# A tail check of tiny weights in place of zeroing them, and a wider spread of the rounding of the four later weights

## The chip, the core and the metric

The kernel runs on one core of one Trainium2 chip. Its engines work in parallel, each through its own queue in a fixed order: TensorE (PE, with its weight loads shown apart as PEld), VectorE (DVE), ScalarE (ACT), GpSimd (POOL), and SyncE (SP), whose queue issues every DMA of this kernel. The metric is the device time of one execution in microseconds (us), the median of the runs.

## The reference

Four batches of 768 positions with 8 heads of width 48 (384 channels) go through three layers, each of which needs the whole output of the one before.

```python
for t in range(S):                                   # gated linear attention
    state = sigmoid(f_logit[:, :, t, :, None]) * state + outer(k[:, :, t], v[:, :, t])
    y[:, :, t] = q[:, :, t] @ state

h = np.maximum(x @ w_in, 0)                          # 384 -> 1024, halves u and v of 512
v_n = (v - mean(v)) / sqrt(var(v) + 1e-06)           # over the 512 channels
gated = u * (w_spatial @ v_n + b_spatial)            # mixes the 768 positions
x = gated @ w_out                                    # 512 -> 384

h = np.maximum(x.T @ w_tok1, 0) @ w_tok2             # token layers, 768 -> 256 -> 768
u = x + h.T
out = u + np.maximum(u @ w_ch1, 0) @ w_ch2           # channel layers, 384 -> 1536 -> 384
```

Six of the weights (`w_in`, `w_out`, `w_tok1`, `w_tok2`, `w_ch1`, `w_ch2`) arrive as 64-bit floats, all else as 32-bit floats. Products are made to nearly full 32-bit precision: each factor is split into a high and a low part, and three matmuls are added up.

## The kernel before

**Stages.** `body` computes everything. For each batch `att` does the attention (scans on DVE, lines 228 to 319; 8 units of two heads a batch, named `pg` and `fkq` by their tiles), `s1` the first product and the normalisation, and `s23` the mixing over positions and the product with `w_out`. The attention of the next batch is woven between the steps of this one (`weave`). After the fourth batch come the token layers (`c1`, `c2`) and the channel layers (`ff`), again batch by batch: `up1` makes 9 matmuls into a PSUM tile, ACT writes its high part `hh` (line 641), DVE its low part `hl` (line 642), and `down` uses both in 9 matmuls (line 654). There are 12 such steps in each of 8 halves, `ff(b, 0)` and `ff(b, 1)`; the latter also has the token layers of the next batch between its steps.

**Rounding the wide weights.** `rounded` (line 58) makes 32-bit floats of a piece of 128 rows by up to 384 columns. A DMA fetches the piece as pairs of 32-bit words (384 KB; line 61, tiles `...st`, ring of three buffers). DVE puts together the new word in two steps (lines 66 and 69), ACT scales the low word (line 73), POOL adds it (line 74). Then ACT squares the high word read as a float (line 75), and DVE multiplies the result with 0 where that square lies under a bound (line 79), so that weights too small for this way of rounding become zero. There are 47 pieces: 9 of `w_in` and 4 of `w_out`, split at once by `split_weight`, and 34 of the four later weights, which `round_weight` writes to a buffer in DRAM (line 93); `split_weight` fetches them again later (line 120, tiles `...sa`).

**The gate.** Attention divides by running products of the gates. Each unit leaves the products in `pend` (line 239). After the last one, DVE takes the least of them (lines 550 to 556) and sets `flag` if it lies under a bound. At the end all engines read the flag; if it is set, `body(True)` does the whole work again in a slower, safe way. With these inputs it is not set.

**Order.** The order of the code is not the order of the queues. Python calls give a stream of instructions; the framework's scheduler then places them by a model of the engines, each as soon as its operands, its buffer and its engine are free there, with code order as a priority. The queues that result are fixed, and an engine that waits for an instruction holds everything behind it.

Of the kernel before, what the change touches and what calls it, by code (L numbers as in the profile page):

```python
# [18 lines left out]
def tile_kernel(ctx, tc, fkqs, v, w_in, w_sp, b_sp, w_out, w_t1, w_t2, w_c1, w_c2, out):  # L19
    nc = tc.nc  # L20
    B, S, DM = v.shape
    P = 128
# [29 lines left out]
    nhalf = const.tile([P, 1], F32, name="nhalf")  # L52
    pend = const.tile([P, B * NP, NCH], F32, name="pend")


    LEAST = 3.4332275390625e-05 ** 2

    def rounded(stage, a, src, c0, width, name):

        st = stage.tile([P, WST, 2], U32, tag="wst", name=f"{name}st")  # L60
        nc.sync.dma_start(
            out=st[:, :width, :].rearrange("p c t -> p (c t)"), in_=src[:, 2 * c0 : 2 * (c0 + width)]
        )
        yield
        lo, hi = st[:, :width, 0], st[:, :width, 1]
        nc.vector.tensor_scalar(
            out=a, in0=hi, scalar1=3, scalar2=0x3FFFFFFF, op0=ALU.logical_shift_left, op1=ALU.bitwise_and
        )
        nc.vector.scalar_tensor_tensor(
            out=a, in0=hi, scalar=0xC0000000, in1=a, op0=ALU.bitwise_and, op1=ALU.bitwise_or  # L70
        )

        nc.scalar.activation(lo, lo, AF.Copy, scale=2.0**-29)
        nc.gpsimd.tensor_tensor(out=a, in0=a, in1=lo, op=ALU.add)
        nc.scalar.activation(f32(hi), f32(hi), AF.Square)
        yield

        a = f32(a)
        nc.vector.scalar_tensor_tensor(out=a, in0=f32(hi), scalar=LEAST, in1=a, op0=ALU.is_ge, op1=ALU.mult)
        return a  # L80

    def round_weight(stage, src, name):

        if src.dtype != mybir.dt.uint64:
            return src, []
        rows, cols = src.shape
        dst = dram.tile([rows, cols], F32, name=name + "d")
        srcr = src.bitcast(U32).rearrange("(n p) c -> n p c", p=P)

        def piece(i, c0, width):  # L90
            at = stage.tile([P, WST], U32, tag="wsa", name=f"{name}da{i}{c0}")
            a = yield from rounded(stage, at[:, :width], srcr[i], c0, width, f"{name}d{i}{c0}")
            nc.sync.dma_start(out=dst[i * P : (i + 1) * P, c0 : c0 + width], in_=a)

        return dst, [
            partial(piece, i, c0, min(WST, cols - c0)) for i in range(rows // P) for c0 in range(0, cols, WST)
        ]

    kept = {}

    def split_weight(pool, stage, src, name, n, cols, eng, first=0, order=None, psum=None):

        wide = src.dtype == mybir.dt.uint64
        h = pool.tile([P, n, cols], F32R, name=name + "h")
        l = pool.tile([P, n, cols], F32R, name=name + "l")
        if wide:
            src = src.bitcast(U32)
        srcr = src.rearrange("(n p) c -> n p c", p=P)

        def piece(i, c0, width):  # L110
            sl = (slice(None), i, slice(c0, c0 + width))
            at = stage.tile([P, WST], U32, tag="wsa", name=f"{name}sa{i}{c0}")
            a = at[:, :width]
            if wide:
                a = yield from rounded(stage, a, srcr[first + i], c0, width, f"{name}{i}{c0}")
                nc.scalar.copy(h[sl], a)
                yield
            else:
                a = f32(a)
                nc.sync.dma_start(out=a, in_=srcr[first + i][:, c0 : c0 + width])  # L120
                yield
                nc.scalar.copy(h[sl], a)
                yield
                yield
            if eng is not nc.tensor:
                eng.tensor_tensor(out=l[sl], in0=a, in1=f32(h[sl]), op=ALU.subtract)
                return

            ps = psum.tile([P, W], F32, tag="m", name=f"{name}pl{i}{c0}")[:, :width]
            nc.tensor.matmul(ps, ident, a, start=True, stop=False)  # L130
            nc.tensor.matmul(ps, minus, h[sl], start=False, stop=True)
            yield
            nc.scalar.copy(l[sl], ps)

        where = [(i, c0, min(WST, cols - c0)) for i in range(n) for c0 in range(0, cols, WST)]
        return h, l, [partial(piece, *x) for x in (order(where) if order else where)]

    def staged(pieces):

        gens = []  # L140

        def step(n):
            if n < len(pieces):
                gens.append(pieces[n]())
            for g in gens[max(0, n - 4) : n + 1]:
                next(g, None)

        return [partial(step, n) for n in range(len(pieces) + 4)]

    def weave(main, *fillers):  # L150

# [14 lines left out]
    def body(general):  # L166
# [12 lines left out]
        wl = lp("wl", 1)  # L179
# [15 lines left out]
        ps_m = lp("ps_m", 3, space=PSUM, st=whole)  # L195
# [10 lines left out]
        first, last = (attp.tile([P, W], F32, name=x) for x in ("first", "last"))  # L206
# [249 lines left out]
        def s23(b):  # L456
# [39 lines left out]


        winh, winl, steps = split_weight(
            wr, wst, w_in, "win", NK, DFF, nc.tensor, order=lambda x: sorted(x, key=lambda y: -y[1]), psum=ps_m
        )  # L500
        weave(att(half(0, 0)), staged(steps))
        bb = const.tile([P, S], F32, tag="bb", name="bb")
        nc.sync.dma_start(out=bb, in_=b_sp.unsqueeze(0).to_broadcast([P, S]))
        wsph, wspl, st_a = split_weight(wl, wst, w_sp, "wsp", NCH, S, nc.tensor, psum=ps_m)
        wouth, woutl, st_b = split_weight(wl, wst, w_out, "wout", NJ, DM, nc.tensor, psum=ps_m)
# [6 lines left out]
        if not general:  # L512
            for name, src in (("wt1", w_t1), ("wt2", w_t2), ("wc1", w_c1), ("wc2", w_c2)):
                kept[name], x = round_weight(wst, src, name)
                early += x
            early = staged(early)
        part = lambda n: early[len(early) * n // 5 : len(early) * (n + 1) // 5]
        for b in range(B - 1):
            if b:
                weave(s1(b, 0), rest)  # L520
            a, rest = s1(b, 1), []
            m, rest = s23(b)
            steps = att(half(b + 1, 0) + half(b + 1, 1))
            cut = len(steps) * len(a) // len(a + m)
            weave(a, steps[:cut], out_steps if b == 0 else part(2 * b - 1))
            weave(m, steps[cut:], part(2 * b))
        right.close()
        wr2 = ExitStack()
        w2p = wr2.enter_context(tc.tile_pool(name="w2p", bufs=1, side="right"))
# [1 line left out]
        t2h, t2l, st_b = split_weight(w2p, wst, kept["wt2"], "wt2", NT1, S, nc.gpsimd)  # L531
        c1h, c1l, st_c = split_weight(w2p, wst, kept["wc1"], "wc1", NK - 1, DC, nc.gpsimd)
        c1w = [(c1h[:, c, :], c1l[:, c, :]) for c in range(NK - 1)]
        weave(rest + s1(B - 1, 0) + s1(B - 1, 1), staged(st_a + st_b))
        conv = st_c
        mid.close()
        w2q = wr2.enter_context(tc.tile_pool(name="w2q", bufs=1, side="right"))
# [10 lines left out]
        if not general:  # L548

            nc.vector.tensor_reduce(  # L550
                out=least, in_=pend.rearrange("p u c -> p (u c)"), op=ALU.min, axis=mybir.AxisListType.X
            )
            row = ps_s.tile([P, W], F32, tag="s", name="row")[:1, :P]
            nc.tensor.transpose(row, least, ident)
            nc.vector.tensor_reduce(out=least[:1], in_=row, op=ALU.min, axis=mybir.AxisListType.X)
            nc.vector.tensor_scalar(out=flag, in0=least[:1], scalar1=LOW, scalar2=None, op0=ALU.is_lt)
# [132 lines left out]
        h3p = e(tc.tile_pool(name="h3p", bufs=4))  # L689
        op = e(tc.tile_pool(name="op", bufs=2))  # L690
        otp = e(tc.tile_pool(name="otp", bufs=3))
        c2h, c2l, st_c = split_weight(w3p, wst, kept["wc2"], "wc2", NF, DM, nc.vector)
        st_c = staged(by_block[2 * NK : 3 * NK] + st_c[:3] + by_block[3 * NK :] + st_c[3:])
        weave(c2(0), st_c[:12])
        for b in range(B):
            more = []
            if b + 1 < B:
                ld, mm = c1(b + 1)
                weave(ff(b, 0), ld, st_c[12:] if b == 0 else [])
                more = mm + c2(b + 1)  # L700
            else:
                weave(ff(b, 0))
            weave(ff(b, 1), more)
        ph2.close()
        wr2.close()
        whole.close()
# [54 lines left out]
```

## Time and profile before

| | us |
|---|---|
| median of three runs | 821.85 (820.16 to 822.72) |
| the profiled execution | 819.0 |
| its span, first to last instruction | 817.2 |

| engine | busy in the span, us | share |
|---|---|---|
| PE | 777.3 | 95% |
| PEld | 716.3 | 88% |
| DVE | 420.3 | 51% |
| ACT | 289.1 | 35% |
| POOL | 211.1 | 26% |

The granted clock of TensorE was 0.978 of full speed over the span. The stages lie about as follows: attention and first layers up to 405 us, the rest of the fourth batch and the first token layers up to 465, channel layers from there to 809. Matmuls are pipelined, so the time of one, as a row prints it, is longer than the distance between two; a busy PE is not PE at its peak. Busy time of weight loads (PEld) shows the density better. A row of the chain of waits names the work that ended last before the next could begin.

### The profile page before, as it was taken

The page shows a single profiled execution, that of the slowest core. Times are in us where ns is not written, and L with a number is a line of the kernel's source. Part 1 is how long each engine was busy: PE and PEld are TensorE (multiplying, and loading weights), DVE is VectorE, ACT ScalarE, POOL GpSimd, SP SyncE. Part 2 cuts the span into 40 slices and gives each one's busy share as a digit, 9 for nine tenths or more (in the row PEclk, how much of TensorE's full clock was granted, in tenths as well). Part 3 has the DMA queues.
Part 4 walks back from the last instruction along what each step waited for, and adds up shares of the span by engine and source line. Part 5 has one row for each costly group of instructions (what it writes and reads, how often), then busy time and mean ns, then how long its engine had stood idle before and what let it go on. Part 6 is the DMA issues. An engine that isn't in the chain of part 4 may idle for free.

```text
span 817.2 us, 12758 instructions
## 1 busy us (share of the span) xinstructions
PE 777.3 (95%) x4860; PEld 716.3 (88%) x4860; DVE 420.3 (51%) x820; ACT 289.1 (35%) x649; POOL 211.1 (26%) x265
## 2 busy tenths in 40 slices
PE   5899899898989999999999999999999999999996
PEld 3577688688779888899899999999999999999995
DVE  6968599899898846673552532122122212221211
ACT  5766464555553444231632531122111211221110
POOL 4524344555641212110760330004000400010000
PEclk9899899999999999999999999999999999999998
DMA  7563435766474321220441410002000200000000
GB/s 254 176 207 104 147 96 164 236 225 214 146 237 140 101 96 59 65 67 24 128 126 40 138 56 30 1 4 85 1 30 0 87 1 30 1 8 24 30 1 33
DMA packets 39847, 73.74 MB, mean 90 GB/s; under 512 B 5216, under 2 KB 29664, under 8 KB 39776
## 3 DMA queue, kind: packets, MB, share of 16 engines
q1 hardware_dynamic: 39776, 72.83, 27.7%
q8 instruction: 40, 0.66, 0.3%
q14 instruction: 31, 0.25, 0.1%
HBM read 54.72 MB, written 15.73 MB: 86 GB/s over the span
## 4 chain that ended last, share of the span: by engine, by line
PE 71%; DVE 10%; DMA 10%; issue 4%; ACT 2%; SPq 1%; POOL 1%; DVEq 0%; ACTq 0%; POOLq 0%
PE po L654 19%; PE p L164 8%; PE p L162 8%; PE p L163 8%; DMA fkq<-in_fkq 3%; PE ps L162 3%; PE ps L164 3%; PE ps L163 3%; PE pa L259 2%; PE py L309 2%; PE py L315 2%; PE px L162 2%; PE px L163 1%; PE px L164 1%; DVE pg L236 1%
## 5 line engine op out<-in xcount | busy, mean ns | idle before, releaser
L642 DVE SCALAR_TENSOR_TENSOR hl<-p,hh 128x384 fp32r<-128x384 f32 x96 | 53.3, 557 | 188.4 <-ACT hh L641 188.4
L641 ACT ACTIVATE hh<-p 128x384 fp32r<-128x384 f32 x96 | 47.2, 492 | 198.0 <-PE p L164 198.0
L654 PE MATMUL po<-hl,wc2h 128*128 128x384 f32 x288 | 97.3, 338 | 0.0
L654 PE MATMUL po<-hh,wc2l 128*128 128x384 f32 x288 | 96.7, 336 | 0.0
L665 POOL TENSOR_TENSOR us<-uh,ul 128x384 f32<-128x384 f32 x24 | 24.3, 1024 | 232.0 <-DVE ul L625 214.7
L654 PE MATMUL po<-hh,wc2h 128*128 128x384 f32 x288 | 75.0, 336 | 0.0
L162 PE MATMUL ps<-wsph,vh 128*128 128x384 f32 x192 | 67.5, 351 | 0.0
L163 PE MATMUL ps<-wspl,vh 128*128 128x384 f32 x192 | 66.4, 346 | 0.0
L164 PE MATMUL ps<-wsph,vl 128*128 128x384 f32 x192 | 66.1, 346 | 0.0
L164 PE MATMUL p<-uh,wc1l 128*128 128x384 f32 x192 | 65.0, 338 | 0.0
L264 POOL TENSOR_SCALAR_AFFINE_SELECT am<-am 128x384 f32<-128x384 f32 x64 | 46.9, 748 | 69.7 <-ACT am L263 69.5
L163 PE MATMUL p<-ul,wc1h 128*128 128x384 f32 x192 | 64.7, 337 | 0.0
L162 PE MATMUL p<-uh,wc1h 128*128 128x384 f32 x192 | 64.2, 338 | 0.0
L654 PEld LDWEIGHTS po<-hl,wc2h 128*128 128x128 f32 x288 | 54.1, 188 | 0.1
L654 PEld LDWEIGHTS po<-hh,wc2l 128*128 128x128 f32 x288 | 54.1, 188 | 0.0
L654 PEld LDWEIGHTS po<-hh,wc2h 128*128 128x128 f32 x288 | 52.3, 188 | 0.0
L236 DVE TENSOR_TENSOR_SCAN pg<-fs,first 128x384 f32<-128x384 f32 x32 | 33.3, 1039 | 22.2 <-ACT first L379 22.1
L259 PE MATMUL pa<-fkq 48*128 48x128 f32 x384 | 40.6, 316 | 3.0 <-ACT am L263 3.0
L259 PEld LDWEIGHTS pa<-fkq 48*128 48x128 f32 x384 | 30.5, 204 | 12.3 <-issue 4.3
L162 PEld LDWEIGHTS ps<-wsph,vh 128*128 128x128 f32 x192 | 37.1, 193 | 2.4 <-issue 1.6
L625 DVE TENSOR_TENSOR ul<-p,uh 128x384 fp32r<-128x384 f32 x24 | 13.4, 557 | 47.6 <-ACT uh L624 47.6
L163 PEld LDWEIGHTS ps<-wspl,vh 128*128 128x128 f32 x192 | 37.0, 193 | 0.5 <-issue 0.2
(419 smaller groups left out, 1928.5 us busy)
## 6 DMA issues: line engine op xcount, KB each, us to landing
fkq<-in_fkq SPq DMA_DIRECT2D x31, 578.0 KB, 4.5
vt<-in_v SPq DMA_DIRECT2D x8, 576.0 KB, 5.9
x1d<-xs SPq DMA_DIRECT2D x24, 192.0 KB, 2.0
xf<-x1d SPq DMA_DIRECT2D x12, 384.0 KB, 4.5
out<-ot SPq DMA_DIRECT2D x24, 192.0 KB, 2.0
wspsa<-in_w_sp SPq DMA_DIRECT2D x12, 192.0 KB, 2.6
wc1d<-wc1da SPq DMA_DIRECT2D x12, 192.0 KB, 2.4
wc2d<-wc2da SPq DMA_DIRECT2D x12, 192.0 KB, 2.2
```

Of the source, the lines that this page charges most:

```text
L162: nc.tensor.matmul(ps, lh, rh, start=first and i == 0, stop=False, **kw)
L163: nc.tensor.matmul(ps, lh, rl, start=False, stop=False, **kw)
L164: nc.tensor.matmul(ps, ll, rh, start=False, stop=i == n - 1, **kw)
L236: nc.vector.tensor_tensor_scan(out=pc, data0=fs[:, :W], data1=first, initial=0.0, op0=ALU.mult, op1=ALU.add)
L259: nc.tensor.matmul(pa[j][:, c, :], ki[64 * j : 64 * j + D, sl], qi[64 * j : 64 * j + D, sl], start=True, stop=True)
L264: nc.gpsimd.affine_select(out=am[j], in_=am[j], compare_op=ALU.is_ge, fill=0.0, base=0, pattern=[[0, NCW], [1, C]], channel_multiplier=-1,)
L309: nc.tensor.matmul(py[:112, c, :], now[c][:112, :112], qi[:112, c * C : (c + 1) * C], start=c == 0, stop=False, skip_group_check=True,)
L315: nc.tensor.matmul(py[64 * j : 64 * j + m, c, :], vt[:, c, h0 + D * j : h0 + D * j + m], am[j][:, c, :], start=False, stop=True, skip_grou ...
L641: nc.scalar.activation(hh, ps, AF.Relu)
L642: nc.vector.scalar_tensor_tensor(out=hl, in0=ps, scalar=0.0, in1=f32(hh), op0=ALU.max, op1=ALU.subtract)
L654: nc.tensor.matmul(po[c], l[:, ft, csl], r, start=ft == 0 and x == 0, stop=ft == NF - 1 and x == 2)
L665: nc.gpsimd.tensor_tensor(out=us[c], in0=f32(uh[:, c, tsl]), in1=f32(ul[:, c, tsl]), op=ALU.add)
```

## The change

- In `body(False)` lines 75 and 79 are left out of all 47 pieces. They stay in `body(True)`, which now also rounds the four later weights anew.
- `look` reads the high words of all 47 pieces once more from the inputs: a DMA into a tile `look` (pool `lkp`, two buffers, 384 KB for most pieces, 256 KB for nine) and on DVE a TENSOR_REDUCE that leaves the least absolute value of each row in a column of `lows`. The code weaves these pieces into `ff(0, 1)` and later halves, up to `ff(2, 1)`.
- `judge` takes the place of lines 550 to 556: it scales `lows`, adds the least of `pend` as a column, and makes the flag of the least of all. The code puts it before the last step of `ff(3, 0)`.
- The 34 pieces of the four later weights were handed over in fifths, from `s23(0)` to `s23(2)`. Now they are handed over in fourteenths, from `s1(1, 1)` to the first layers of the fourth batch.

```diff
-    def rounded(stage, a, src, c0, width, name):
+    def rounded(stage, a, src, c0, width, name, tiny):
...
         nc.gpsimd.tensor_tensor(out=a, in0=a, in1=lo, op=ALU.add)
-        nc.scalar.activation(f32(hi), f32(hi), AF.Square)
+        if tiny:
+            nc.scalar.activation(f32(hi), f32(hi), AF.Square)
         yield
-
         a = f32(a)
-        nc.vector.scalar_tensor_tensor(out=a, in0=f32(hi), scalar=LEAST, in1=a, op0=ALU.is_ge, op1=ALU.mult)
+        if tiny:
+
+            nc.vector.scalar_tensor_tensor(
+                out=a, in0=f32(hi), scalar=LEAST**2, in1=a, op0=ALU.is_ge, op1=ALU.mult
+            )
         return a
...
+    def look(stage):
...
+        def piece(n, src, c0, width):
+            st = stage.tile([P, WST, 2], U32, tag="look", name=f"look{n}")
+            nc.sync.dma_start(
+                out=st[:, :width, :].rearrange("p c t -> p (c t)"), in_=src[:, 2 * c0 : 2 * (c0 + width)]
+            )
+            yield
+            nc.vector.tensor_reduce(
+                out=lows[:, n : n + 1], in_=f32(st[:, :width, 1]), op=ALU.min, axis=mybir.AxisListType.X,
+                apply_absolute_value=True,
+            )
...
-        part = lambda n: early[len(early) * n // 5 : len(early) * (n + 1) // 5]
+        part = lambda n, m: early[len(early) * n // 14 : len(early) * m // 14]
         for b in range(B - 1):
             if b:
-                weave(s1(b, 0), rest)
+                weave(s1(b, 0), rest, part(7 * b - 9, 7 * b - 7) if b > 1 else [])
...
-            weave(a, steps[:cut], out_steps if b == 0 else part(2 * b - 1))
-            weave(m, steps[cut:], part(2 * b))
+            weave(a, steps[:cut], out_steps if b == 0 else part(7 * b - 7, 7 * b - 5))
+            weave(m, steps[cut:], part(7 * b - 5, 7 * b - 2) if b else [])
...
-        weave(rest + s1(B - 1, 0) + s1(B - 1, 1), staged(st_a + st_b))
+        weave(rest + s1(B - 1, 0) + s1(B - 1, 1), staged(st_a + st_b), part(12, 14))
...
+        def judge():
+
+            nc.vector.tensor_scalar(
+                out=lows[:, :NLOW], in0=lows[:, :NLOW], scalar1=LOW / NEAR, scalar2=None, op0=ALU.mult
+            )
             nc.vector.tensor_reduce(
-                out=least, in_=pend.rearrange("p u c -> p (u c)"), op=ALU.min, axis=mybir.AxisListType.X
+                out=lows[:, NLOW : NLOW + 1], in_=pend.rearrange("p u c -> p (u c)"), op=ALU.min,
+                axis=mybir.AxisListType.X,
             )
+            nc.vector.tensor_reduce(out=least, in_=lows, op=ALU.min, axis=mybir.AxisListType.X)
...
+        lkp = e(tc.tile_pool(name="lkp", bufs=2))
...
+        looks = [] if general else staged(look(lkp))
+        part = lambda n: looks[len(looks) * n // (2 * B - 3) : len(looks) * (n + 1) // (2 * B - 3)]
         for b in range(B):
...
-                weave(ff(b, 0), ld, st_c[12:] if b == 0 else [])
+                weave(ff(b, 0), ld, st_c[12:] if b == 0 else part(2 * b - 1))
...
-                weave(ff(b, 0))
-            weave(ff(b, 1), more)
+                weave(ff(b, 0), [] if general else [judge])
+            weave(ff(b, 1), more, part(2 * b) if b + 1 < B else [])
```

What the scheduler makes of it stands in the queues. First DVE during the second batch, where pieces of `w_ch2` (`wc2d...`, after the change `wc20d...`) are rounded between the scans and the normalisation. Before:

```order
L66 TENSOR_SCALAR wc2da_3619<-wc2d60st 128x384
L69 SCALAR_TENSOR_TENSOR wc2da_3619<-wc2d60st,wc2da_3619 128x384
L66 TENSOR_SCALAR wc2da_3629<-wc2d70st 128x384
L69 SCALAR_TENSOR_TENSOR wc2da_3629<-wc2d70st,wc2da_3629 128x384
L79 SCALAR_TENSOR_TENSOR wc2da_3619<-wc2d60st,wc2da_3619 128x384
L66 TENSOR_SCALAR wc2da_3721<-wc2d80st 128x384
L295 COPY z_2434<-pk_2426 112x48
L391 TENSOR_TENSOR xl_2104<-py_2334,xh_2103 112x384
L69 SCALAR_TENSOR_TENSOR wc2da_3721<-wc2d80st,wc2da_3721 128x384
L79 SCALAR_TENSOR_TENSOR wc2da_3629<-wc2d70st,wc2da_3629 128x384
```

The same place after the change:

```order
L67 TENSOR_SCALAR wc20da_3589<-wc20d20st 128x384
L70 SCALAR_TENSOR_TENSOR wc20da_3589<-wc20d20st,wc20da_3589 128x384
L67 TENSOR_SCALAR wc20da_3663<-wc20d30st 128x384
L70 SCALAR_TENSOR_TENSOR wc20da_3663<-wc20d30st,wc20da_3663 128x384
L67 TENSOR_SCALAR wc20da_3777<-wc20d40st 128x384
L70 SCALAR_TENSOR_TENSOR wc20da_3777<-wc20d40st,wc20da_3777 128x384
L463 BN_STATS bs_2042<-r_2040 128x6
L67 TENSOR_SCALAR wc20da_3822<-wc20d50st 128x384
L465 BN_AGGR mv_2044<-bs_2042 128x2
L70 SCALAR_TENSOR_TENSOR wc20da_3822<-wc20d50st,wc20da_3822 128x384
```

A piece has two steps on DVE in place of three. The place itself has hardly moved: counted in scans and normalisations that stand ahead, 32 of the 34 later pieces are rounded where they were or slightly earlier, in the first and second batch; the last two of `w_ch2` alone went to the fourth batch.

Second, DVE in `ff(0, 0)`, with one `hl` a step. Before:

```order
L642 SCALAR_TENSOR_TENSOR hl_5397<-p_5386,hh_5396 128x384
L642 SCALAR_TENSOR_TENSOR hl_5421<-p_5410,hh_5420 128x384
L642 SCALAR_TENSOR_TENSOR hl_5445<-p_5434,hh_5444 128x384
L642 SCALAR_TENSOR_TENSOR hl_5489<-p_5478,hh_5488 128x384
L675 TENSOR_TENSOR ot_5469<-po_5176,us_5219 128x384
```

After, some steps earlier in the same half:

```order
L118 TENSOR_REDUCE lows<-look_5953 128x1
L118 TENSOR_REDUCE lows<-look_5981 128x1
L118 TENSOR_REDUCE lows<-look_6007 128x1
L678 SCALAR_TENSOR_TENSOR hl_5251<-p_5240,hh_5250 128x384
L118 TENSOR_REDUCE lows<-look_6059 128x1
L118 TENSOR_REDUCE lows<-look_6085 128x1
L678 SCALAR_TENSOR_TENSOR hl_5277<-p_5266,hh_5276 128x384
L118 TENSOR_REDUCE lows<-look_6111 128x1
L118 TENSOR_REDUCE lows<-look_6140 128x1
L678 SCALAR_TENSOR_TENSOR hl_5302<-p_5291,hh_5301 128x384
```

All 47 reductions stand between `c2(0)` and the eighth step of `ff(0, 1)`, most of them two or three to a step; 9 stand ahead of the fifth `hl` of `ff(0, 0)`, 37 between it and the eighth `hl` of `ff(0, 1)` (six of these of the 256 KB kind), one behind that.

Third, SP at the end of `ff(0, 0)`. Before, the outputs follow the fetches of `w_ch2`:

```order
L120 DMA wc2sa_5306<-wc2d 128x384
L120 DMA wc2sa_5333<-wc2d 128x384
L676 DMA out<-ot_5469 128x384
L676 DMA out<-ot_5472 128x384
L676 DMA out<-ot_5475 128x384
```

After, they stand between fetches of `look`:

```order
L114 DMA look_6480<-in_w_c 128x768
L114 DMA look_6506<-in_w_c 128x768
L114 DMA look_6544<-in_w_c 128x768
L712 DMA out<-ot_5374 128x384
L712 DMA out<-ot_5377 128x384
L114 DMA look_6582<-in_w_c 128x768
L712 DMA out<-ot_5380 128x384
L114 DMA look_6617<-in_w_c 128x768
```

Every fetch of `look` waits there until the reduction two pieces earlier has freed its buffer.

## Rows read from the trace of the kernel before

**Rows 1.** The page: the chain that ended last, by engine, over the span.
```profile
PE 71%; DVE 10%; DMA 10%; issue 4%; ACT 2%; SPq 1%; POOL 1%; DVEq 0%; ACTq 0%; POOLq 0%
```

**Rows 2.** Busy time in four stretches (us, instructions), granted clock, DMA share, GB/s.
```profile
0.00:100.00 100.00, 81.10 (x559) 59.50 (x560) 75.69 (x151) 61.37 (x149) 38.06 (x66) 0.93 0.57 180
100.00:250.00 150.00, 139.20 (x903) 119.51 (x902) 136.13 (x272) 78.05 (x180) 75.98 (x86) 0.94 0.56 183
250.00:410.00 160.00, 157.97 (x1099) 139.50 (x1098) 98.70 (x208) 61.88 (x144) 40.73 (x70) 1.00 0.28 85
410.00:820.00 410.00, 399.05 (x2304) 397.81 (x2303) 109.75 (x190) 87.84 (x176) 56.29 (x45) 0.99 0.11 36
```

**Rows 3.** The chain in 250 to 300 us by line, then its pieces from 224 us.
```profile
by line: PE px L162 9.3%; PE ps L163 8.4%; PE ps L164 8.4%; PE ps L162 8.4%; PE px L163 7.7%; PE pa L259 7.7%; PE py L315 7.6%; PE px L164 7.3%; PE py L309 7.0%; PE pv L164 4.6%; PE pv L163 4.2%; PE pv L162 4.1%; PE pu L162 3.1%; PE pu L163
...
224.29 1.19 DVE wc2da L79
225.48 0.02 issue
225.50 0.33 SPq L93
...
225.94 4.13 DMA wc2d70st<-in_w_c
...
230.16 0.51 DVE wc2da L66
```

**Rows 4.** Line 79 alone: its busy time on DVE in two stretches.
```profile
0.00:100.00 100.00, 7.13 (x12) 0.93 0.57 180
100.00:250.00 150.00, 21.19 (x34) 0.94 0.56 183
```

**Rows 5.** Steps of DVE in the channel layers: start, us, instruction, idle time before.
```profile
478.50 1.01 DVE L642 SCALAR_TENSOR_TENSOR hl<-p,hh 128x384 fp32r<-128x384 f32 x2
481.50 0.56 DVE L642 SCALAR_TENSOR_TENSOR hl<-p,hh 128x384 fp32r<-128x384 f32 x1 [2.00 <-ACT hh L641]
484.67 0.56 DVE L642 SCALAR_TENSOR_TENSOR hl<-p,hh 128x384 fp32r<-128x384 f32 x1 [2.61 <-ACT hh L641]
...
531.63 0.56 DVE L642 SCALAR_TENSOR_TENSOR hl<-p,hh 128x384 fp32r<-128x384 f32 x1 [2.61 <-ACT hh L641]
```

**Rows 6.** Matmuls of PE around one step of the channel layers.
```profile
480.60 0.34 PE L164 MATMUL p<-uh,wc1xl 128*128 128x384 f32 x1
...
484.82 0.69 PE L654 MATMUL po<-hh,wc2h 128*128 128x384 f32 x3
...
485.52 0.35 PE L654 MATMUL po<-hl,wc2h 128*128 128x384 f32 x1
```

**Rows 7.** DMA issues of line 61: count, KB, us from issue to landing.
```profile
win20st<-in_w_in SPq DMA_DIRECT2D x1, 384.0 KB, 4.0
...
wout30st<-in_w_out SPq DMA_DIRECT2D x1, 384.0 KB, 3.1
...
wc2d50st<-in_w_c SPq DMA_DIRECT2D x1, 384.0 KB, 3.0
...
wt1d50st<-in_w_t SPq DMA_DIRECT2D x1, 256.0 KB, 2.5
```

**Rows 8.** Busy time in three stretches of the channel layers, columns as in rows 2.
```profile
456.00:479.00 23.00, 23.00 (x138) 22.83 (x136) 13.96 (x22) 12.68 (x26) 15.19 (x12) 1.00 0.48 155
479.00:501.00 22.00, 22.00 (x127) 21.91 (x126) 4.35 (x9) 3.46 (x7) 0.00 (x0) 1.00 0.00 1
501.00:537.00 36.00, 36.00 (x210) 35.89 (x210) 8.80 (x17) 6.37 (x13) 3.03 (x3) 1.00 0.05 17
```

**Rows 9.** The only TENSOR_REDUCE on 128 rows: nanoseconds, start, shapes.
```profile
L550 DVE TENSOR_REDUCE least<-pend x1: 254/254/254, 360.2 to 360.2; 128x1 f32<-128x96 f32 x1
```

**Rows 10.** Two neighbouring stretches early on, columns as in rows 2.
```profile
30.00:35.00 5.00, 2.47 (x27) 1.83 (x28) 5.00 (x9) 3.82 (x9) 3.22 (x3) 0.93 0.48 160
35.00:40.00 5.00, 5.00 (x15) 2.51 (x17) 5.00 (x10) 3.94 (x10) 2.46 (x4) 0.50 0.61 179
```

More of the change, by code (lines that the diff above doesn't have):

```diff
@@ L53, in tile_kernel @@
     pend = const.tile([P, B * NP, NCH], F32, name="pend")
-    LEAST = 3.4332275390625e-05 ** 2
-    def rounded(stage, a, src, c0, width, name):
+    LEAST = 3.4332275390625e-05
+    NEAR = 3.5e-05
+    def rounded(stage, a, src, c0, width, name, tiny):
         st = stage.tile([P, WST, 2], U32, tag="wst", name=f"{name}st")
@@ L74, in rounded, with round_weight @@
         nc.gpsimd.tensor_tensor(out=a, in0=a, in1=lo, op=ALU.add)
-        nc.scalar.activation(f32(hi), f32(hi), AF.Square)
+        if tiny:
+            nc.scalar.activation(f32(hi), f32(hi), AF.Square)
         yield
         a = f32(a)
-        nc.vector.scalar_tensor_tensor(out=a, in0=f32(hi), scalar=LEAST, in1=a, op0=ALU.is_ge, op1=ALU.mult)
+        if tiny:
+            nc.vector.scalar_tensor_tensor(
+                out=a, in0=f32(hi), scalar=LEAST**2, in1=a, op0=ALU.is_ge, op1=ALU.mult
+            )
         return a
-    def round_weight(stage, src, name):
+    def round_weight(stage, src, name, tiny):
         if src.dtype != mybir.dt.uint64:
@@ L91, in piece @@
             at = stage.tile([P, WST], U32, tag="wsa", name=f"{name}da{i}{c0}")
-            a = yield from rounded(stage, at[:, :width], srcr[i], c0, width, f"{name}d{i}{c0}")
+            a = yield from rounded(stage, at[:, :width], srcr[i], c0, width, f"{name}d{i}{c0}", tiny)
             nc.sync.dma_start(out=dst[i * P : (i + 1) * P, c0 : c0 + width], in_=a)
@@ L99, in tile_kernel, with split_weight @@
     kept = {}
-    def split_weight(pool, stage, src, name, n, cols, eng, first=0, order=None, psum=None):
+    wides = [w for w in (w_in, w_out, w_t1, w_t2, w_c1, w_c2) if w.dtype == mybir.dt.uint64]
+    NLOW = sum(w.shape[0] // P * -(-w.shape[1] // WST) for w in wides)
+    lows = const.tile([P, NLOW + 1], F32, name="lows")
+    def look(stage):
[9 more added lines that the diff above has]
+            )
+        out = []
+        for w in wides:
+            wr = w.bitcast(U32).rearrange("(n p) c -> n p c", p=P)
+            for i in range(w.shape[0] // P):
+                for c0 in range(0, w.shape[1], WST):
+                    out.append(partial(piece, len(out), wr[i], c0, min(WST, w.shape[1] - c0)))
+        assert len(out) == NLOW
+        return out
+    def split_weight(pool, stage, src, name, n, cols, eng, first=0, order=None, psum=None, tiny=False):
         wide = src.dtype == mybir.dt.uint64
@@ L114, in piece @@
             if wide:
-                a = yield from rounded(stage, a, srcr[first + i], c0, width, f"{name}{i}{c0}")
+                a = yield from rounded(stage, a, srcr[first + i], c0, width, f"{name}{i}{c0}", tiny)
                 nc.scalar.copy(h[sl], a)
@@ L498, in body @@
         winh, winl, steps = split_weight(
-            wr, wst, w_in, "win", NK, DFF, nc.tensor, order=lambda x: sorted(x, key=lambda y: -y[1]), psum=ps_m
+            wr, wst, w_in, "win", NK, DFF, nc.tensor, order=lambda x: sorted(x, key=lambda y: -y[1]), psum=ps_m,
+            tiny=general,
         )
@@ L504, in body @@
         wsph, wspl, st_a = split_weight(wl, wst, w_sp, "wsp", NCH, S, nc.tensor, psum=ps_m)
-        wouth, woutl, st_b = split_weight(wl, wst, w_out, "wout", NJ, DM, nc.tensor, psum=ps_m)
+        wouth, woutl, st_b = split_weight(wl, wst, w_out, "wout", NJ, DM, nc.tensor, psum=ps_m, tiny=general)
         s10, a01, sa = s1(0, 0), att(half(0, 1)), staged(st_a)
@@ L511, in body @@
         early = []
[L512 to L516, printed above, removed]
-        part = lambda n: early[len(early) * n // 5 : len(early) * (n + 1) // 5]
+        for name, src in (("wt1", w_t1), ("wt2", w_t2), ("wc1", w_c1), ("wc2", w_c2)):
+            kept[name], x = round_weight(wst, src, f"{name}{int(general)}", general)
+            early += x
+        early = staged(early)
+        part = lambda n, m: early[len(early) * n // 14 : len(early) * m // 14]
         for b in range(B - 1):
             if b:
-                weave(s1(b, 0), rest)
+                weave(s1(b, 0), rest, part(7 * b - 9, 7 * b - 7) if b > 1 else [])
             a, rest = s1(b, 1), []
@@ L546, in body @@
         h1p = wr2.enter_context(tc.tile_pool(name="h1p", bufs=1, side="right"))
-        if not general:
+        def judge():
+            nc.vector.tensor_scalar(
+                out=lows[:, :NLOW], in0=lows[:, :NLOW], scalar1=LOW / NEAR, scalar2=None, op0=ALU.mult
+            )
             nc.vector.tensor_reduce(
-                out=least, in_=pend.rearrange("p u c -> p (u c)"), op=ALU.min, axis=mybir.AxisListType.X
+                out=lows[:, NLOW : NLOW + 1], in_=pend.rearrange("p u c -> p (u c)"), op=ALU.min,
+                axis=mybir.AxisListType.X,
             )
+            nc.vector.tensor_reduce(out=least, in_=lows, op=ALU.min, axis=mybir.AxisListType.X)
             row = ps_s.tile([P, W], F32, tag="s", name="row")[:1, :P]
```

## The prediction

> **What bounds the kernel now.** I read the chain of waits first, since a share of busy time averages over stages. Over the span PE holds 71% of it, DVE and DMA 10% each [rows 1]; the question is where DVE and DMA hold it. The table of stretches tells [rows 2]: from 100 to 250 us DVE is busy 136.13 of 150 us and PE's weight loads only 119.51; from 250 to 410 DVE falls to 98.70 of 160 and the weight loads reach 139.50, a density of 0.872. The chain in 250 to 300 is all PE [rows 3]. Just before, at 224 to 230 us, it runs through the rounding: L79 on DVE (1.19), the write-back (0.33), the load of the piece that takes the buffer (4.13 from 225.94, so until 230.07), and at 230.16 L66 on DVE. So the first 250 us are bound by DVE and the ring of three buffers, the rest by PE. In the channel layers PE is busy 399.05 of 410 us, and DVE only 109.75 [rows 2].
>
> **The change: what goes.** L79 is busy 7.13 us (12 pieces) up to 100 us and 21.19 us (34) up to 250, where it stands on the bounding engine [rows 4]. L75 goes with it; ACT, busy 61.37 and 78.05 us in these stretches [rows 2], does not bound them, but the square is a step between a landed load and its free buffer, so the ring turns faster too. What is late next is PE. In 100 to 250 us its 119.51 us of weight loads would at the density of the next stretch take 119.51 / 0.872 = 137 us. That gives 13 us of the 21.19; all 21 could come only if the clock, 0.94 there and 1.00 in the next stretch, rose too. Up to 100 us DVE is busy but 75.69 of 100, so I count half of the 7.13, 3.5. Sum 16.5, say 17; bounds 8 (60% of the 13, nothing in front) and 26 (all of 21.19 and 5 in front).
>
> [...]
>
> **What moves.** The handing-over in fourteenths has next to no effect: in the order, 32 of the 34 later pieces stay where they were or come slightly earlier, since the scheduler starts a piece when a buffer is free. Two pieces of `w_ch2` go to the fourth batch, where DVE has 61 of 160 us free [rows 2]: nothing. The judge's few steps in the last half stand beside DVE's waits of 2.61 us a step [rows 5], and its flag is there some 40 us before the end. Formerly they stood near 360 us (L550 at 360.2, 254 ns [rows 9]), where PE bounds: nothing again.
>
> **What is added.** 47 loads and 47 reductions on DVE. Their busy time is nothing (DVE is busy 4.35 of 22 us in a stretch of these steps [rows 8]); their place is something. DVE works in order, two or three reductions stand ahead of each `hl`, and each waits for its load, which waits on SP for the reduction two pieces earlier. So what counts is the turn of one of the two buffers:
>
> - landing: 3.0 to 3.1 us for 384 KB in `wc2d50st` and `wout30st`, 4.0 in `win20st`, 2.5 for 256 KB [rows 7]. I take 3.05, for DMA is idle in this stretch (0.00 and 0.05 [rows 8]), while 3.0 was reached in one at 0.56 [rows 2];
> - waking DVE: 230.16 - 230.07 = 0.09, say 0.1 [rows 3];
> - the reduction of 384 elements: no row has it. The nearest rows are 254 ns for 96 elements [rows 9], a floor, and 0.56 for a two-operand step of 384 [rows 5], a ceiling. I take 0.55, the row of the same width;
> - the next issue on SP: 0.02, as the issue step in the chain [rows 3].
>
> That is 3.72 us a turn, and with two buffers 1.86 us a look; the small ones take 3.05 - 2.5 = 0.55 less, 1.57 or so. The bounds of a look are 1.71 (reduction of 0.25) and 2.33 (landing of 4.0).
>
> In the order 37 looks stand between the fifth `hl` of `ff(0, 0)` (478.50 [rows 5], the second of the two in that row) and the eighth of `ff(0, 1)` (531.63), 53.1 us of PE's own pace. Two of the 37 are already loaded; the rest are 29 large and 6 small: 29 x 1.86 + 6 x 1.57 = 63.4, and about 1 for the two waiting reductions: 64.5. So the eighth `hl` comes 11.4 us late. An `hl` has slack: it ends at 481.50 + 0.56 = 482.06 and PE, which ends the next step's first product at 480.60 + 0.34, takes it at 485.52 after `hh` [rows 5, 6], 3.46 later. So PE loses 8 us, and behind the last look nothing gives it back, PE being the bound. The bounds: at 1.71 a look 3.5 to 4; at 2.33 (small ones 1.9) 80 us, or 23 lost. The nine looks ahead of them fall into a stretch where the weights' own loads hold DMA to 0.48 [rows 8]; I add nothing, as they are spread over more than 20 us. Outputs queued between looks on SP go out a few us late, which nobody waits for; the loads of the next token layers stand behind them too, and are fetched ahead of their use.
>
> **The sum.** 17 less 8 is 9. The profiled execution took 819.0 (span 817.2), so 810; the median of the runs stands 2.85 above it, so 821.85 - 9 = 813.
>
> **The rivals.**
>
> *The looks cost nothing* (0.13). For it: DMA is all but idle there [rows 8], so two loads at once might land well under 3 us, and with the reduction at its floor and 3.46 us of slack the looks just keep PE's pace: that needs a look at (53.1 + 3.46 - 1 - 9) / 29 = 1.6 us. Against it: no load of this size landed under 3.0 [rows 7]. Then 821.85 - 17 = 805.
>
> *The looks pace the channel layers and cost more than the front gives* (0.21), the other side. The same ring, one price higher: two looks in flight land at 4.0 like `win20st` [rows 7] or 4.13 like `wc2d70st` [rows 3], a look takes 2.33 us, and PE loses 23. [...] With 13 of relief the sum is +10, 832; with 17 it is 828. It decides from the point where the cost exceeds 17: 53.1 + 3.5 + 17 = 73.6 us for the looks, less 1 and 6 x 1.8, by 29: 2.13 us a look (2.0 where the relief is 13).
>
> *The front gives less* (0.14). By the matmuls PE is idle only 10.8 of the 150 us [rows 2], and the stages up to 100 us, where attention's own scans and loads set the pace, give nothing. Then 10.8 less 8: about 819, within 0.3% or just beyond. Against it: the share of the matmuls goes from 0.928 to 0.987 between the two stretches, that of the weight loads from 0.797 to 0.872, so PE gets more done in a busy us, too, when DVE does not hold it.
>
> *The change doesn't do what it says.* For the handing-over this is what I forecast; it is in no sum.
>
> **How the numbers follow.** My forecast, 813, has 0.52; its own range is 806 to 819 (relief and cost at their middle bounds). About 0.3%, 2.5 us, can be told from no change, so faster is below 819.4 and slower above 824.3. Faster: nearly all of the forecast (0.47), the free looks (0.13) and a little of the third rival: 0.62. Slower: the second rival and a bit of the forecast's tail: 0.22. The rest is 0.16. The range goes to the free looks at one end with some more relief, 801, and into the second rival at the other, 830.
>
> **What would show it.** Relief: the first step of the channel layers comes 15 to 18 us earlier in the profile after; DVE's busy time in 100 to 250 us is lower by some 20, weight loads are denser, and the chain there passes to PE. If it comes less than 11 us earlier, the step from weight-load density was wrong. Looks: TENSOR_REDUCE on `look` about 1.86 us apart, each after an idle DVE ended by its load; `hl` no longer released by `hh` but behind a reduction; idle PE of about 1 us a step, released by `hl`, about 8 us in sum; a clock still near 1.00. If PE waits 15 us or more there, the landing in the idle stretch was mis-sized; if none, the slack was. I would be wholly wrong if chain time moved to somewhere that I hold free: the outputs and loads behind the looks on SP, or the fourth batch.

## The result, and the profile after

The changed kernel takes 830.59 us (median of 12 runs, 824.91 to 836.25) against 820.03 for the kernel before (12 runs): a ratio of 1.0129, 95% interval 1.0098 to 1.0160. It is slower by 10.6 us; the forecast was 813, faster. The time lies 0.6 us beyond the upper end of the forecast's range, 830, and within the 828 to 832 that the second rival gave. The profiled execution took 833.0 us, with a span of 831.3.

The page of after: the chain that ended last by engine and by line, and the group of the new reductions.

```profile
PE 64%; DMA 19%; DVE 9%; issue 3%; SPq 2%; POOL 2%; ACT 1%; DVEq 0%; POOLq 0%
PE po L690 15%; PE p L195 6%; PE p L194 6%; PE p L193 6%; DMA look<-in_w_c 5%; PE ps L193 4%; PE ps L195 3%; PE ps L194 3%; PE pa L290 3%; DMA fkq<-in_fkq 3%; DMA look<-in_w_in 3%; PE py L340 2%; PE py L346 2%; DMA xh<-yh 2%; DMA look<-in_w_t 2%
...
L118 DVE TENSOR_REDUCE lows<-look 128x1 f32<-128x384 f32 (+1 forms) x47 | 24.7, 526 | 51.3 <-DMA look<-in_w_c 29.7
```

DMA's part of the chain rose from 10% [rows 1] to 19%; loads of `look` hold 10% of the span in it. The 47 reductions take 0.526 us each, but DVE stood idle 51.3 us ahead of them.

Busy time in stretches, after (columns as in rows 2), and then the row of before for 460 to 550 us:

```profile
0.00:100.00 100.00, 83.51 (x554) 60.11 (x555) 69.17 (x139) 56.44 (x137) 37.09 (x65) 0.91 0.56 175
100.00:250.00 150.00, 139.09 (x945) 118.11 (x945) 124.82 (x253) 64.20 (x152) 65.94 (x85) 0.99 0.62 196
250.00:410.00 160.00, 158.53 (x1092) 140.15 (x1091) 95.04 (x195) 62.51 (x144) 44.75 (x73) 1.00 0.27 83
...
460.00:550.00 90.00, 76.96 (x398) 72.21 (x398) 41.49 (x78) 18.10 (x37) 11.45 (x8) 0.94 0.71 205
```

```profile
460.00:550.00 90.00, 90.00 (x525) 89.63 (x524) 28.68 (x47) 22.67 (x47) 14.97 (x12) 1.00 0.12 40
```

From 460 to 550 us PE now makes 398 matmuls in place of 525. The 127 that are missing would take 21.8 us at the pace of before. PE is idle 13.0 of the 90 us, and the granted clock is 0.94, which is worth some 5 us (6% of the 90, an estimate). These two make 18 of the 22 us; in the rest PE counts as busy at a lower density (72.21 us of weight loads to 76.96 of matmuls, before 89.63 to 90.00). From 100 to 250 us, where rows 2 show DVE at 136.13, it is at 124.82 and 42 more matmuls are done.

Three points show where the time goes. The rows give a line's start on DVE, first to last: the first token layer (`h1l`) and the channel layers (`hl`), before and then after.

```profile
L591 DVE SCALAR_TENSOR_TENSOR h1l<-p,h1h x8: 557/558/558, 449.0 to 695.4; 128x384 fp32r<-128x384 f32 x8
...
L642 DVE SCALAR_TENSOR_TENSOR hl<-p,hh x96: 544/558/560, 465.7 to 806.5; 128x384 fp32r<-128x384 f32 x96
```

```profile
L627 DVE SCALAR_TENSOR_TENSOR h1l<-p,h1h x8: 547/558/558, 443.7 to 711.6; 128x384 fp32r<-128x384 f32 x8
...
L678 DVE SCALAR_TENSOR_TENSOR hl<-p,hh x96: 542/557/559, 464.7 to 822.2; 128x384 fp32r<-128x384 f32 x96
```

After is 5.3 us ahead at the first `h1l`, only 1.0 at the first `hl`, and 15.7 behind at the last: some 21 us are lost in the stretch with the looks. (What lies ahead of the first `h1l` is called the front here. Its first 60 us differ between executions: in this profile the clock was 0.75 from 30 to 60 us, in that of before 0.89. So the front is read from medians and from several profiles, below, not from this one.)

The chain in that stretch, after, in order of time (start, us, what):

```profile
467.25 7.85 DMA look<-in_w_in
...
479.91 0.55 DVE lows L118
...
501.57 3.24 DMA look<-in_w_c
504.83 0.56 DVE lows L118
505.41 3.73 DMA look<-in_w_c
509.16 0.56 DVE lows L118
509.75 3.42 DMA look<-in_w_c
513.18 0.56 DVE lows L118
...
547.83 3.39 DMA look<-in_w_c
551.24 0.55 DVE lows L118
551.79 0.47 DVE hl L678
```

Load, reduction, load into the same buffer, reduction: from 479.91 us on the ring of two buffers is the whole chain, for 72 us. From 501.57 to 551.79 it makes 12 turns in 50.2 us, 4.19 us each, or 2.09 us a look. How that reaches PE is seen on DVE and in what PE waits for, after:

```profile
504.83 0.55 DVE L118 TENSOR_REDUCE lows<-look 128x1 f32<-128x384 f32 x1 [1.38 <-DMA look<-in_w_c]
505.30 0.55 DVE L678 SCALAR_TENSOR_TENSOR hl<-p,hh 128x384 fp32r<-128x384 f32 x1
506.79 0.55 DVE L118 TENSOR_REDUCE lows<-look 128x1 f32<-128x384 f32 x1 [0.95 <-DMA look<-in_w_c]
509.16 0.55 DVE L118 TENSOR_REDUCE lows<-look 128x1 f32<-128x384 f32 x1 [1.82 <-DMA look<-in_w_c]
509.63 0.55 DVE L678 SCALAR_TENSOR_TENSOR hl<-p,hh 128x384 fp32r<-128x384 f32 x1
```

```profile
PE po L690 <- DVE hl L678: 8.0, 10, 1.6
PE p L195 <- DVE h1l L627: 1.9, 1, 1.9
PE po L690 <- DVE ot L711: 1.8, 1, 1.8
PE po L690 <- ACT hh L677: 1.6, 1, 1.6
```

Here `hl` waits for nothing of its own any more (rows 5 have 2.61 us of idle time before it, released by `hh`); it goes right behind a reduction, these two 4.3 us apart in place of 3.17. PE waits for `hl` 10 times, up to 1.6 us (the columns are us in total, times, longest). The `h1l` and the `ot` that it waits for stand behind reductions on DVE too, at 529.22 and 512.00 us. The kernel before has no such wait in this stretch.

### The profile page after: what moved, and what is told of

Read it like the earlier page. It is cut to its first block, busy times and chain, and to the rows that moved or that the text cites. A ratio compares the mean times of both kernels' runs of the same rounds, so it can differ in the third digit from the quotient of the medians.

```text
span 831.3 us, 12758 instructions
## 1 busy us (share of the span) xinstructions
PE 782.5 (94%) x4860; PEld 713.2 (86%) x4860; DVE 418.3 (50%) x822; ACT 268.6 (32%) x602; POOL 202.9 (24%) x265
## 4 chain that ended last, share of the span: by engine, by line
PE 64%; DMA 19%; DVE 9%; issue 3%; SPq 2%; POOL 2%; ACT 1%; DVEq 0%; POOLq 0%
PE po L690 15%; PE p L195 6%; PE p L194 6%; PE p L193 6%; DMA look<-in_w_c 5%; PE ps L193 4%; PE ps L195 3%; PE ps L194 3%; PE pa L290 3%; DMA fkq<-in_fkq 3%; DMA look<-in_w_in 3%; PE py L340 2%; PE py L346 2%; DMA xh<-yh 2%; DMA look<-in_w_t 2%
## 5 line engine op out<-in xcount | busy, mean ns | idle before, releaser
L690 PE MATMUL po<-hl,wc2h 128*128 128x384 f32 x288 | 99.2, 344 | 8.1 <-DVE hl L678 8.0
L690 PE MATMUL po<-hh,wc2h 128*128 128x384 f32 x288 | 77.4, 345 | 3.4 <-DVE ot L711 1.8
L295 POOL TENSOR_SCALAR_AFFINE_SELECT am<-am 128x384 f32<-128x384 f32 x64 | 41.6, 665 | 99.6 <-ACT am L294 99.4
L118 DVE TENSOR_REDUCE lows<-look 128x1 f32<-128x384 f32 (+1 forms) x47 | 24.7, 526 | 51.3 <-DMA look<-in_w_c 29.7
L340 PE MATMUL py<-fkq,state 112*112 112x128 f32 x160 | 33.3, 302 | 6.2 <-DVE state L315 6.2
```

Source lines behind the costliest of these rows:

```text
L118: nc.vector.tensor_reduce(out=lows[:, n : n + 1], in_=f32(st[:, :width, 1]), op=ALU.min, axis=mybir.AxisListType.X, apply_absolute_value=True,
L295: nc.gpsimd.affine_select(out=am[j], in_=am[j], compare_op=ALU.is_ge, fill=0.0, base=0, pattern=[[0, NCW], [1, C]], channel_multiplier=-1,)
L340: nc.tensor.matmul(py[:112, c, :], now[c][:112, :112], qi[:112, c * C : (c + 1) * C], start=c == 0, stop=False, skip_group_check=True,)
L690: nc.tensor.matmul(po[c], l[:, ft, csl], r, start=ft == 0 and x == 0, stop=ft == NF - 1 and x == 2)
```

## The experiments

Each kernel was timed beside the kernel before on the same chip. The median of before was 820.0 us beside after, 817.8 to 818.9 beside the others. The ratio is the one on record; it differs from the quotient of the two medians by up to 0.3%.

| run | median, us | ratio to before, 95% |
|---|---|---|
| after | 830.6 | 1.0129 (1.0098 to 1.0160) |
| e1 without looks | 806.4 | 0.987 (0.982 to 0.992) |
| e2 no zeroing | 813.0 | 0.9935 (0.990 to 0.997) |
| e3 looks only | 836.5 | 1.021 (1.017 to 1.026) |
| e4 one look a step | 806.9 | 0.985 (0.980 to 0.989) |
| e5 four buffers | 810.9 | 0.987 (0.982 to 0.992) |
| e6 small looks | 807.0 | 0.983 (0.979 to 0.987) |
| e7 one step of rounding | 801.9 | 0.977 (0.973 to 0.981) |
| e8 handing-over only | 818.6 | 0.998 (0.995 to 1.000) |
| e9 no zeroing, handing-over | 810.0 | 0.992 (0.988 to 0.995) |
| e10 no zeroing, late flag | 814.0 | 0.995 (0.992 to 0.997) |

**The two halves apart: e1 and e3.** In e1 the looks are gone, and the flag goes by `pend` alone:

```diff
-        looks = [] if general else staged(look(lkp))
+        looks = []
```

> The kernel after without the 47 looks: the flag goes by the attention's products alone, so the test for tiny weights is left out. Theory A (front small, looks dear): attention and first layers are only some 5.5 us earlier, as the trace of after shows near 450 us, and nothing takes it back: 814 to 816 against 820 of the kernel before. Theory B (front as predicted, 17 us, but the looks or what goes with them already disturb the stretch ahead of 450 us): 803 to 806.

It came out at 806.4, 11.4 us under before, between the two theories and within 0.4 us of theory B; the interval reaches from 6 to 15 us. In its profile the first `h1l` starts at 437.8, 11.2 us ahead of before, and the lead stays to the end. So theory A's 5.5 us, read from a single profile of after, was too small. Theory B's reason falls as well. After, e1, e4, e5 and e6 have the same front, and in none is a look issued ahead of the first `h1l`; yet that step is 5.3, 11.2, 6.5, 5.5 and 13.2 us ahead of before. At the 25th scan, which starts at 107.63 in before, the five already differ: -0.7, 4.1, -1.4, -1.9 and 4.6 us. So the profile of after had a slow front by execution, not by the looks.

e3 is the kernel before with `look`, its pool and its places in the weave added:

```diff
+        lkp = e(tc.tile_pool(name="lkp", bufs=2))
...
+        looks = [] if general else staged(look(lkp))
...
-            weave(ff(b, 1), more)
+            weave(ff(b, 1), more, part(2 * b) if b + 1 < B else [])
```

> The kernel before with the 47 looks added, zeroing kept, their results unused. Order on DVE around the looks is that of the kernel after. Theory A: a turn of a buffer takes 4.0 us and the first ones over 4.4 us, so the looks alone cost 20 to 23 us: 840 to 843. Prediction (turn of 3.72 us, 8 us lost): 828. If under 835, the looks of the kernel after suffer from something that the new front brings.

836.5, so 18.7 us for the looks alone (interval 14 to 21), where nothing else changed. In its profile the last `hl` is 23.0 us late, of which 2.9 stood there at the first `h1l` and 7.1 at the first `hl`. That is a little less than theory A, and not the 8 us of the prediction. The halves add up: a ratio of 0.987 and one of 1.021 make 1.008 for the whole, which within their intervals is the 1.013 measured.

**Density or number: e4.** Each load is tied to a step of the channel layers, by one element that ACT copies into the buffer from the newest `hh`:

```diff
+            nc.scalar.copy(f32(st[:, :1, 0]), f32(latest[0][:, :1]))
             nc.sync.dma_start(
...
+                latest[0] = hh
```

> The kernel after, each load of a look tied to a step of the channel layers: a one-element copy on ACT from the newest hh into the buffer stands ahead of the load. So the planner can no longer draw the looks early, and their reductions stand about one a step from the second half on. Theory A (the cost is the pace of the ring with two or three looks ahead of each hl): a turn of 4.0 us of one buffer of two is 2.0 us a look against steps of 3.17 us, PE waits little, 814 to 818. Rival (each look costs on its own, since DVE stands still for a load of 3.5 us whatever their density): up to 1 us for each of the 47, 830 or more.

806.9: the looks cost nothing that can be seen (e1 has 806.4; in the profile the lead is 6.5 us at the first `h1l` and 7.2 at the last `hl`), with the same 47 loads and the same 47 reductions on the same DVE. Theory A's 814 to 818 missed since it reckoned with a front of 5.5 us. This kernel does all that after does and is 11 us faster than before. Its reductions run from 497.7 to 708.8 us in place of 452.8 to 553.3. A stretch of its DVE:

```profile
555.13 0.55 DVE L120 TENSOR_REDUCE lows<-look 128x1 f32<-128x384 f32 x1 [1.06 <-DMA look<-in_w_out]
557.46 0.55 DVE L120 TENSOR_REDUCE lows<-look 128x1 f32<-128x384 f32 x1 [1.78 <-DMA look<-in_w_out]
557.93 0.55 DVE L680 SCALAR_TENSOR_TENSOR hl<-p,hh 128x384 fp32r<-128x384 f32 x1
560.15 0.56 DVE L680 SCALAR_TENSOR_TENSOR hl<-p,hh 128x384 fp32r<-128x384 f32 x1 [1.67 <-ACT hh L679]
564.16 0.42 DVE L120 TENSOR_REDUCE lows<-look 128x1 f32<-128x256 f32 x1 [3.45 <-DMA look<-in_w_t]
564.49 0.55 DVE L680 SCALAR_TENSOR_TENSOR hl<-p,hh 128x384 fp32r<-128x384 f32 x1
```

DVE still stands idle for a load, up to 3.45 us, but then the next step is free of it, and the slack takes it up: from 445 to 800 us the profile has no wait of PE for another engine. The rival, a price for each look, falls. (The looks also begin 45 us later here, behind the loads of `w_ch2`; e5 and e6 leave them early and dense.)

**The price of a turn: e5 and e6.** e5 has `bufs=4` for `lkp`. e6 fetches 48 columns of each piece.

> The kernel after with four buffers for the looks in place of two. The planner uses them to pack the looks tighter: 37 of them now stand between the fifth hl of ff(0, 0) and the fifth of ff(0, 1), 12 steps or 39 us of PE's pace. If a landing of 3.5 us is a latency, four at once give one look a us, which keeps up: 806 to 810, as without looks. If it is shared rate (two at once move 384 KB in 2.0 us, about 190 GB/s; the most in any slice of the page is 267), a look takes 1.5 to 1.6 us, 55 to 59 us for the 37, PE loses 13 to 17 and some more ahead of them: 820 to 827.

> The kernel after, but a look fetches and tests only 48 columns of its piece, 48 KB (so seven eighths of the weights are not tested). The planner packs them tighter still, three to five a step. If the landing is mostly fixed (192 KB take 2.0 us by the page), a turn is near 2.3 us, 1.2 us a look, and the 32 looks of nine steps (28.5 us) take 38: 6 us lost, 812 to 816. If it is mostly size, the landing falls under 1 us and nothing is lost: 805 to 808.

The landings of the most frequent load, as the DMA rows give them (count, KB, median us): after, then e4, e5 and e6.

```profile
look<-in_w_c SPq DMA_DIRECT2D x24, 384.0 KB, 3.5
```

```profile
look<-in_w_c SPq DMA_DIRECT2D x24, 384.0 KB, 3.1
```

```profile
look<-in_w_c SPq DMA_DIRECT2D x24, 384.0 KB, 4.4
```

```profile
look<-in_w_c SPq DMA_DIRECT2D x24, 48.0 KB, 1.7
```

A load that is mostly alone lands in 3.1 us, two in flight in 3.5, four in 4.4. So both theories for e5 were half right: the rate is shared, yet four in flight still pay. A turn of 4.4 + 0.55 by four is 1.24 us a look. This is a stretch of e5:

```profile
480.00:500.00 20.00, 20.00 (x116) 20.00 (x115) 11.25 (x23) 3.47 (x7) 0.00 (x0) 1.00 0.91 303
```

It moved 303 GB/s, more than the 267 that I had taken as a ceiling, and PE is busy throughout. At 37 looks the turn makes 46 us. The profile has 45.7 from the fifth `hl` of `ff(0, 0)` to the fifth of `ff(0, 1)`, where before has 42.3 (the 39 of the expectation left out the token layers between them). These 3.4 us are no more than the slack of 3.5, and PE waits for `hl` once, 1.9 us. What e5's profile does lose lies ahead of that: the lead of 5.5 us at the first `h1l` is 2.5 at the first `hl`. The median, 810.9, lies near the latency theory and 4.5 us above that of e1, but both have a ratio of 0.987 to the kernel before beside them, so the times do not tell e5 from e1.

In e6 the turn is 1.7 + 0.21 us, 0.96 a look. The packing got denser, PE still waits 2.4 us for `hl`, and the lead goes from 13.2 us at the first `h1l` to 9.4 at the last `hl`. The landing is mostly fixed, as the first theory for e6 had it, but the time, 807.0, is that of the second. It cannot tell e6 from e1.

**The front: e2, e7, e8, e9, e10.** e2 takes the two steps out of before and changes nothing else:

```diff
-        nc.scalar.activation(f32(hi), f32(hi), AF.Square)
...
-        nc.vector.scalar_tensor_tensor(out=a, in0=f32(hi), scalar=LEAST, in1=a, op0=ALU.is_ge, op1=ALU.mult)
```

> The kernel before with the square on ACT and the multiplication on DVE taken out of all 47 pieces and nothing else (old handing-over in fifths, flag where it was; tiny weights are neither zeroed nor tested). Theory A1: the handing-over does nothing, so the same as the kernel after without looks, 814 to 816. Theory A2: the handing-over in fourteenths costs the front, and here the relief is 10 us or more: 810 or less. Prediction: 803 to 806.

It came out at 813.0, so the zeroing alone is worth 4.8 us (interval 3 to 8), between the two theories. e1, which also has the handing-over in fourteenths and the late flag, is at 806.4. Three runs were to tell which of the two makes the 6.6 us: e8 is before with the `part` lines of the diff, e9 is e2 with them, e10 is e2 with the flag made in `ff(3, 0)`.

> The kernel before with the handing-over of the 34 later pieces in fourteenths, all else as it was (zeroing kept, no looks). Prediction (the scheduler starts a piece when a buffer is free, wherever it is handed over): 817 to 820, no change. Theory H (the 6.6 us between the kernel after without looks and the one before without zeroing are the handing-over's own): 810 to 814.

> The kernel before without the zeroing (both steps, all 47 pieces) and with the handing-over in fourteenths; the flag stays near 360 us, no looks, no test for tiny weights. Theory I (the handing-over is worth nothing with the zeroing, but 5 to 7 us without it): as the kernel after without looks, 805 to 808. Theory J (the late flag, or only where the few steps around 395 us fall, makes that difference): as without zeroing alone, 811 to 814.

> The kernel before without the zeroing and with the flag made in the last half, as after; handing-over in fifths, no looks, no test for tiny weights. Theory I: the late flag is worth nothing, 811 to 814. Theory J: the five steps of the flag near 360 us hold the fourth batch up, and without them 805 to 808.

By itself the handing-over does nothing (818.6 beside 818.9), nor does the late flag on e2 (814.0). Handing-over on e2 gives 810.0, between the theories, with an interval that overlaps that of e2 and the upper part of e1's. So it may be worth some 3 us once the zeroing is gone, and the rest of the 6.6 stays open; e4 and e6, which have both, lie with e1. The profiles show one place: from 390 to 410 us PE waits 2.0 us in e2 and 0.8 in e1, and the clock is 0.95 and then 0.88 in e2, 1.00 in e1. What makes that difference is not shown.

e7 is e1 with only the load, line 67 and the write-back left of the 34 later pieces.

> The kernel after without looks, and of the rounding of the 34 later weights only the load, the first step on DVE and the write-back left (the second step on DVE and the steps on ACT and POOL are left out, so these weights are wrong). Theory F1 (the rounding, DVE and its ring of three buffers, still bounds the front, which is why the relief was 11 and not 17): 3 to 8 us faster than without looks, 798 to 803. Theory F2 (the front is by then bound by attention's own loads and PE): 804 to 808.

Theory F1: 801.9, 4.5 us under e1 (a ratio to before of 0.977 in place of 0.987). The row of the stretch where most of that rounding lies, e1 and then e7:

```profile
100.00:250.00 150.00, 138.74 (x964) 118.45 (x963) 127.28 (x259) 63.56 (x150) 65.05 (x83) 0.99 0.60 192
```

```profile
100.00:250.00 150.00, 145.18 (x986) 125.32 (x985) 101.56 (x227) 50.58 (x121) 24.59 (x51) 0.97 0.60 197
```

Without the zeroing DVE is still busy 127.28 of 150 us, only 8.9 less than in rows 2, where 21.19 us of L79 [rows 4] went: other work moved up. PE makes 964 matmuls there in place of 903 [rows 2]. When more of the rounding goes it makes 986, and the weight loads get denser, 125.32. So the rounding of the later pieces goes on bounding the front. e7 takes out its steps on DVE, ACT and POOL together and does not tell which of them.

## Why the prediction was wrong

**The step that failed is the price of a turn, 3.72 us, and with it the 8 us for the looks.** They cost 18.7 us (e3) at a turn of 4.19. The other term of the sum, the relief of 17, was too large as well (e1: 11), but 11 less 8 would still have been faster. The mechanism of the looks was the right one: two buffers, two or three reductions ahead of each `hl`, loss of PE time from the fifth `hl` on. From there to the eighth of `ff(0, 1)` I counted 64.5 us; the profile of after has 551.79 - 479.05 = 72.7. (The fifth `hl` is the first of the two at 478.50 in rows 5, not the second; the time was right.) Two things were under-sized, and a third was left out:

- *The landing.* I took 3.05 us, the lowest of the rows of line 61, because the stretch was idle. But the looks end that idleness: DMA's share there went from 0.12 to 0.71. With two in flight a load takes 3.5. e4 shows that 3.05 was right for a load alone. With 3.5 in place of 3.05 the same working gives 0.22 us a look more, some 8 us for 35 looks: the whole miss between these two `hl`.
- *The looks ahead of it.* I added nothing for the nine that stand earlier, as they are spread over more than 20 us. They share DMA and SP with the loads of `w_ch2` and with each other: 4.4 us is the median landing of the looks at `w_in`, one took 7.85, and DVE held `ul`, `wc2l` and `hl` behind them. The loads of `w_ch2` (`wc2sa`) land in 3.9 us in place of 2.9 (medians), and ACT stood idle 2.64 and 1.92 us for two of them ahead of `uh` and `hh`. The lead of 5.3 us at the first `h1l` was 1.0 at the first `hl`: 4.3 us for what was put at nothing. e3 has 4.2.
- *The clock.* Over 460 to 550 us it was 0.94, and the forecast had not reckoned with that, though in rows 10 it is 0.50 right behind 5 us in which PE was busy 2.47. The 6% that are missing give away 5 of the 90 us, an estimate, but this adds little here: from 479.91 to 551.79 us the chain has no PE in it, so a faster PE would have waited longer. The 8 and the 4.3 us above, on top of the 8 that were forecast, already make 20 of the 21 that were lost. The rows of after that answer to rows 10 (PE busy 2.41 of 5 us, then 0.66 of the clock):

```profile
460.00:465.00 5.00, 2.41 (x13) 1.75 (x12) 2.75 (x6) 2.27 (x6) 1.51 (x2) 1.00 0.92 261
465.00:470.00 5.00, 4.68 (x19) 4.68 (x20) 3.62 (x8) 1.59 (x4) 2.14 (x2) 0.66 0.92 279
```

The prediction's own signs read as follows. PE's waits for `hl` came to 8.0 us, the very sum that was forecast, and yet the looks cost more than twice that: with the waits for `h1l`, `ot` and `hh` PE lost 13.3 us, to which come the clock and the thinner matmuls. The first step of the channel layers came 11.1 us earlier in e1, not 15 to 18; in after, where the looks stand ahead of it, 1.0.

The deciding point of the second rival was 2.13 us a look, or 2.0 where the relief is 13. The measured look was 2.09 and the relief smaller still, so it decided as the rival said.

**The relief** was forecast at 17, with 8 to 26 as bounds, for the zeroing alone. e1, with the whole new front, measured 11; e2, the zeroing alone, 4.8, which is under the lower bound. The 3.5 us up to 100 us can't be told from the profiles (at 108 us the five with the new front lie from 1.9 us behind to 4.6 ahead). From there to the first `h1l` they gain 6.0 to 8.6 us, e1 7.1, where the density of the weight loads had promised 13. The step that failed there is that PE is late next: with L79 gone DVE was filled at once by the steps behind it, and e7 shows 4.5 us more in the rest of the rounding. The reckoning also took busy time for work. A weight load of 128x128 takes 0.19 us at a clock of 1.00 and 0.33 in after at 465.81 us, where the clock had fallen (0.50 from 465.5 to 466.5 us); so the 119.51 us of weight loads [rows 2] were stretched by a clock of 0.94, and in after 118.11 us at 0.99 made 42 matmuls more. The count of matmuls would have been the better measure. That the whole relief of e1 is near the third rival's 10.8 is luck: that rival put all of it at 100 to 250 us and nothing ahead.

**What held.** The handing-over alone moves nothing, as forecast from the order (e8), though it may be worth some 3 us without the zeroing, which I had not seen. The late flag costs nothing (e10). The reduction was taken at 0.55 us; the rows have 0.552 for 384 elements and 0.419 for 256 (after), 0.203 for 48 (e6). The outputs that stand between looks on SP landed in 3.8 to 5.1 us at the end of `ff(0, 0)`, before in 1.9 to 2.0, and nobody waited for them. The first rival's free looks did come about, in e4, by another order and not by shorter landings.

**The chances.** 0.21 for the other side was too little. The forecast gained 17 and lost 8 with the lower end of one price and the middle of another; the 38 loads of 384 KB of line 61 landed in 3.0 to 5.8 us, and with their median, 3.8, in place of the lowest a look takes 2.24 us, the looks cost 21 and the sum is +4.

## What to carry to other kernels

A transfer that is added to an idle stretch is no longer in an idle stretch (here DMA's share went from 0.12 to 0.71): price it with as many in flight as the ring allows (3.5 us with two and 4.4 with four, 3.1 mostly alone), and by the middle of the rows, not by the best one (3.8 against 3.0). Spare time on an engine that works in order helped here only as long as the instruction at the head of its queue didn't wait. DVE was half idle (busy 50% of the span of after), and 47 short reductions cost some 20 us because two or three of them stood ahead of each step that PE waits for, each with a load that came every 2.09 us. The same 47, at about one a step, cost nothing (e4), and at 1.24 us a look, still packed, some 4 us at most (e5). When an instruction is taken off the engine that bounds a stretch, ask which work of its own queue moves up before asking what the next engine can take.

## What the hardware showed that was not expected

Four loads of 384 KB in flight reached 303 GB/s over 20 us with 4.4 us a landing (e5), two of them 200 GB/s from 500 to 552 us with 3.5 (after). One that is mostly alone takes 3.1 (e4), and one of 48 KB, with two in flight, takes 1.7 (e6). A line through these last two, an estimate, has some 1.5 us that do not depend on size: (3.1 - 1.7) / 336 KB is 4.2 ns a KB, 0.2 us for 48 KB.
